# Packed attention and gated feed-forward on one core: a new order of all five queues, and another split of the low-part subtractions between VectorE and GpSimd

## The chip, the cores and the metric

The kernel runs on 1 core of one Trainium2 chip. Its engines are PE (TensorE matmul; PEld is its weight load), DVE (VectorE), ACT (ScalarE), POOL (GpSimd) and SP (SyncE, which issues nearly all DMAs). The metric is the device time of one execution in microseconds (us).

## The reference

Batch 8, 8 heads, 576 rows, head width 64. A pack of 32 queries per head attends to k and v, then every row of q attends to the 32 packed rows; the rows of all heads, 512 wide, go through a feed-forward layer with a gate.

```
p_packed = softmax(p k^T / 8) v          # 32 rows per head
x        = softmax(q p_packed^T / 8) p_packed   # 4608 x 512 over all batches
h        = x @ w_in                      # 512 -> 2048
g        = h * clip(h + 3, 0, 6) / 6
out      = g @ w_out                     # 2048 -> 512
```

The two weights arrive as 64-bit floats, which the kernel reads as pairs of 32-bit words and puts together on the core; q, k, v and p are 32-bit floats.

## The kernel before, in words

**Precision.** A product of two 32-bit matrices is made of three matmuls of rounded parts: high times high, high times low, low times high. So every operand has a high part, which ACT makes by a copy into the rounded type, and a low part, the operand minus its high part, which DVE or POOL makes by a subtraction. `parts_of` (lines 1036 to 1041) issues both, and the table ENGINES names the engine of each subtraction: "D" for DVE, "P" for POOL, and the default of the caller where the table has no entry.

```
def parts_of(hi, lo, x, name, engine="P"):
    nc.scalar.copy(out=hi, in_=x)
    yield
    on(name, engine).tensor_sub(out=lo, in0=x, in1=hi.bitcast(F32))
    yield
```

**Stages.** The start loads k, v, q and p of batch 0 and turns them on PE, makes both attentions of batch 0, and meanwhile reads the weights. Line 404 and line 406 (ACT), line 410 (DVE) and line 414 (POOL) put the two words of a weight block together, 512 columns at a time. The attention comes out as `a_hi` (line 950, ACT) and `a_lo` (line 952, DVE or POOL) for two groups of heads; w_in times the packed rows comes out as `m_hi` and `m_lo` (lines 483 and 485). The first product of the feed-forward layer of batch 0 is line 747: for one block f of 128 hidden units 12 matmuls of 288 columns, six with the parts of group 0 and six with those of group 1, into one pair of PSUM banks (`ps_h`). Only one block has room there at a time: block f+1 starts when the gate of block f has read the banks, by ACT (line 1581, relu of h + 3) and DVE (line 1583, the minimum with 6 times h). The second product is line 997.

Batches 1 to 7 follow. A batch has two halves of 256 or 320 rows. In a half the 16 hidden blocks go in pairs: two first products (line 1019, 6 matmuls each, into one of two PSUM banks in turn), then 7 second products of 3 matmuls each (line 997), which use sums and differences of blocks to save an eighth of the products. Between them stands the gate of each block: line 1030 (ACT) and line 1032 (DVE) read the bank of h and so set it free for the first product after next; then come sums and differences on DVE (lines 1184, 1197, 1203), the high parts on ACT (line 1039) and the low parts on DVE or POOL (line 1041), in the tiles `ge`, `gf`, `ga`. A strip at the edge of a half is kept by POOL (line 1052) and worked off by halves of their own in batches 3 and 7. Beside this the attention of the next batch runs: transposes of q and k on DVE (line 737), scores on PE (line 1347), softmax on ACT and DVE (lines 692 to 714 and 1440), and w_in times the packed rows (line 1449, parts on lines 1455 and 1457). The end of a half combines four accumulators (lines 1233, 1236, 1239, 1246) and stores the rows.

**What sets the order.** Every piece of work is a chain of steps, written as a generator; one step issues one instruction or one group of them. The strings PLAN (batch 0 and the start) and PLANS (batches 1 to 7) name the chain of the next step, word by word: in PLAN `h0` is the first product of block 0, `r0` its gate, `a1` a step of reading w_in for block 1; in PLANS `p14` is a step of pair 4 of the second half, `a14` and `b14` its gates, `z0` a softmax step. Each engine runs its own instructions in the order of that text, so the words also set the order on all five queues. HOMES names the buffer that each tile of four kinds takes.

Of the kernel before, what the change touches and what calls it, by code (L numbers as in the profile page):

```python
# [48 lines left out]
b0 b0 b0 x0 x0 a4 m2 x0 a5 a5 y0 x0 r1 r1 a6 a4 a4 a4 lk0 b6 tk0 li7 m2 m2 m2 r1 r1 a7 a7 a7 h2 h2 a6 a6 y0 x1
a7 x1 r2 r2 x1 lo3 lk1 tk1 h3 h3 b3 a6 r2 r2 tp y2 b5 b5 b5 b5 m4 lk2 y2 x2 b3 b3 b3 r3 x2 tk2 m4 r3 y3 y3 x1  # L50
m4 m4 m4 h4 h4 b5 b5 lo4 b4 li8 r3 r3 b6 b6 b6 li10 x2 b3 b3 r4 r4 a10 x3 x3 x3 a10 a8 lk3 tk3 S b4 b4 x2 x3
a10 S S S S lo8 S h5 h5 b4 below S S b4 b4 r4 li9 r4 y4 y4 y1 y1 x4 x4 lo9 a10 b6 b6 lq0 li11 x4 S S b8 a8 a8
r5 y5 x4 b8 r5 b8 h6 h6 b9 r5 a8 r5 b8 a9 a9 x5 a9 a9 x5 x5 x5 lo7 r6 y6 r6 y6 lq2 h7 h7 a11 a11 a11 b9 y5 tq2
b7 b7 tq0 b7 r6 r6 r7 b8 y7 a11 m8 r7 y7 b8 lo12 b7 m8 m8 m8 b7 S r7 m8 x6 x6 x6 S S S S h8 h8 r8 b9 r7 li13
a13 a13 lq1 tq1 li12 x6 y8 b7 lo10 r8 b9 b9 a13 a13 r8 r8 a12 x7 x7 h9 h9 r9 r9 E E a12 y9 y9 lw0 x7 x7 E a12
b9 b10 b10 y8 E E lq3 li14 a12 tq3 b10 r9 S h10 h10 r10 y10 x8 b10 a14 r10 E E r9 x8 x8 b12 b12 S h11 a14 a14
lv h11 x8 r11 r11 a14 lw1 V r10 x9 b12 b12 b10 y11 V V y11 T T x9 b10 li15 a15 a15 a15 Z Z Z Z Z x9 a15 x9 Z
m12 lo11 b11 b11 b11 r10 x10 b11 m12 m12 m12 y10 m12 lo13 x10 h12 h12 r11 r11 b12 b12 b11 b11 lo14 r12 x10 x10
# [22 lines left out]
-m2 -p12 -b11 -o0 -o0 -p12 -a11 -a11 -p10 -p10 -z0 -b10 -z0 -a12 -a12 -p10 -p10 -p10 -p10 -p10 -p13 -z0 -m2
-a12 -m2 -b12 -z0 -b11 -b11 -b11 -p11 -p11 -m2 -b11 -b11 -b11 -t3 -b11 -z0 -b12 -t1 -a12 -b12 -t3 -t3 -t3 -t3
-t3 -w1 -o0 -p13 -p11 -p11 -p11 -p11 -p11 -a13 -b12 -m2 -z1 -b13 -b12 -b12 -a13 -p12 -b12 -b12 -b12 -s18 -a12
-p12 -b12 -p12 -p12 -a13 -p12 -p12 -p12 -z1 -a13 tk1 -t4 -z1 -g18 -g18 -g18 -a13 -p13 -z1 -b13 -s19 -b13 -m1
-t4 -t4 -g18 -t2 -b13 -b13 -b13 -b13 -b13 -p13 -p13 -z1 -g19 -g19 -m1 -t4 -z1 -b13 -m1 -m1 -b13 -m1 -g19 -s111
-g111 -s110 -t3 -t3 -p13 -g19 -p13 -z1 -p13 -o1 -t4 -t4 -g111 lk0 tk0 -g110 -s18 -g110 -p13 -s113 -w0 -s18 -t5
-t5 -t4 -t4 lq1 -s112 -s19 -s19 -g110 -g110 -o1 -g111 -t5 -t5 -g112 -g112 -t5 -m0 -g112 -s114 -t5 -g111 -z1
-g112 -t5 -s110 -s111 -s110 -m0 -m0 -s111 -t5 -g114 -g114 -z0 -g113 -z0 -o1 -g113 -g113 -s115 -t4 -t4 p05 -t5
-g113 lk2 tk2 -g114 -s112 -s113 -t5 -t5 -t4 a05 -s112 -s113 -t5 -m0 -m0 -g114 -w3 -g115 -g115 -g115 p05 a05
a05 -t5 p04 a05 -o1 -o1 -t5 -t5 -t5 lk3 b05 b05 a05 b05 -s114 -g115 a04 a04 -t5 b05 b05 -s115 a04 -m3 -o1 -t5  # L90
# [1633 lines left out]
```

## Time and profile before

| | |
|---|---|
| Runs | 724.3, 729.7, 723.89 us; median 724.3 |
| Profiled execution | 723.53 us, its span 721.7 us |
| PE busy | 686.5 us, 95% of the span |
| DVE busy | 616.9 us, 85% |
| ACT busy | 433.3 us, 60% |
| POOL busy | 279.7 us, 39% |
| Mean granted clock of PE | 0.986 of full speed |

Busy time is a share of the span; what lies around the span in the profiled execution is 723.53 - 721.7 = 1.8 us. A busy time does not tell whether the work lies on the path that sets the end: that is read from which engine the others wait for in a stretch. The rows are further below.

### The profile page before, as it was taken

The numbers are of one execution on the slowest core, as the hardware profiler recorded it, in microseconds if no ns is written. First come the engines' busy times: TensorE is split into PE (matmuls) and PEld (weight loads), VectorE is DVE, ScalarE is ACT, GpSimd is POOL, SyncE is SP. The second block draws the span as 40 slices with busy tenths as digits, with TensorE's granted clock in tenths as the row PEclk, the third lists the DMA queues.
The fourth block names the chain that finished last, engine by engine and source line by source line (L and its number), as shares of the span: only waits on it lengthen the run. The fifth ranks groups of instructions, "written<-read, shape, count | busy, mean of one in ns | idle before, by whom it ended". The sixth has DMA issues, their size and how long they took to land.

```text
span 721.7 us, 17048 instructions
## 1 busy us (share of the span) xinstructions
PE 686.5 (95%) x6142; PEld 601.1 (83%) x6142; DVE 616.9 (85%) x1495; ACT 433.3 (60%) x1062; POOL 279.7 (39%) x434
## 2 busy tenths in 40 slices
PE   6399999999999999999999999999999999999997
PEld 4277877776878888898998998898989879999996
DVE  2878879699999899979988979997999889788795
ACT  3778966655656556565655656654556655655553
POOL 0345753343322443444323234354322343444332
PEclk9879999999999999999999999999999999999999
DMA  9979942886867459676866875978685845424642
GB/s 224 311 172 238 226 137 74 218 209 203 282 159 190 152 193 298 127 189 189 248 225 178 174 222 173 255 151 213 222 266 122 178 172 193 189 90 151 228 153 82
DMA packets 209156, 138.48 MB, mean 192 GB/s; under 512 B 174256, under 2 KB 186800, under 8 KB 205232
## 3 DMA queue, kind: packets, MB, share of 16 engines
q1 hardware_dynamic: 208800, 137.33, 67.1%
q8 instruction: 48, 0.79, 0.5%
q14 instruction: 36, 0.29, 0.1%
q10 hardware_dynamic: 272, 0.07, 0.0%
HBM read 115.34 MB, written 22.02 MB: 190 GB/s over the span
## 4 chain that ended last, share of the span: by engine, by line
PE 54%; DVE 27%; DMA 6%; ACT 5%; issue 4%; POOL 1%; SPq 1%; DVEq 0%; POOLq 0%; ACTq 0%
PE acc L997 29%; PE h L1019 15%; PE ps_h L747 3%; DVE t L1032 3%; PE at L1449 3%; DVE tr L737 2%; DMA room<-in_q_dram 2%; DVE tb L1032 1%; DVE t L1197 1%; DVE ga L1041 1%; PE at L1347 1%; DVE osb L1239 1%; DVE gf L1041 1%; DVE t L1184 1%; DMA e_again<-e_kept 1%
## 5 line engine op out<-in xcount | busy, mean ns | idle before, releaser
L1019 PE MATMUL h<-a_hi,m_hi 128*128 128x320 f32 (+1 forms) x448 | 138.3, 309 | 6.1 <-DVE t L1032 4.2
L1019 PE MATMUL h<-a_lo,m_hi 128*128 128x320 f32 (+1 forms) x448 | 132.6, 296 | 0.2 <-DVE a_lo L714 0.2
L1019 PE MATMUL h<-a_hi,m_lo 128*128 128x320 f32 (+1 forms) x448 | 132.6, 296 | 0.0
L1019 PEld LDWEIGHTS h<-a_hi,m_hi 128*128 128x128 f32 x448 | 84.8, 189 | 25.9 <-DVE t L1032 10.3
L997 PE MATMUL acc<-wo_hi,ge 128*128 128x256 f32 x456 | 105.8, 283 | 0.1
L997 PE MATMUL acc<-wt,ga 128*128 128x256 f32 x684 | 105.5, 284 | 0.0
L1030 ACT ACTIVATE t<-h,three 128x256 f32<-128x256 f32 (+1 forms) x126 | 63.1, 502 | 56.6 <-PE h L1019 32.5
L997 PEld LDWEIGHTS acc<-wt,ga 128*128 128x128 f32 x684 | 91.9, 191 | 2.8 <-issue 1.7
L1019 PEld LDWEIGHTS h<-a_lo,m_hi 128*128 128x128 f32 x448 | 85.0, 190 | 1.0 <-DVE a_lo L714 0.5
L1019 PEld LDWEIGHTS h<-a_hi,m_lo 128*128 128x128 f32 x448 | 84.7, 189 | 0.3 <-DVE m_lo L1457 0.3
L997 PEld LDWEIGHTS acc<-wo_hi,ge 128*128 128x128 f32 x456 | 80.6, 189 | 5.0 <-issue 2.5
L1039 ACT CAST ga<-t 128x256 fp32r<-128x256 f32 (+1 forms) x114 | 48.1, 422 | 35.4 <-PE acc L997 14.1
L1041 POOL TENSOR_TENSOR ge<-t,ge 128x256 fp32r<-128x256 f32 x57 | 44.9, 788 | 57.1 <-ACT ge L1039 49.8
L1030 ACT ACTIVATE tb<-h,three 128x256 f32<-128x256 f32 (+1 forms) x98 | 49.1, 501 | 29.8 <-PE h L1019 22.7
L1032 DVE SCALAR_TENSOR_TENSOR t<-t,h 128x256 f32<-128x256 f32 (+1 forms) x126 | 55.9, 446 | 12.8 <-ACT t L1030 12.3
L1041 POOL TENSOR_TENSOR ga<-t,ga 128x256 fp32r<-128x256 f32 (+1 forms) x51 | 41.0, 803 | 62.2 <-ACT ga L1039 54.2
L997 PE MATMUL acc<-wo_lo,ge 128*128 128x256 f32 x228 | 63.9, 280 | 0.0
L997 PE MATMUL acc<-wt,gf 128*128 128x256 f32 x342 | 60.3, 285 | 0.2 <-DVE osb L1246 0.2
L997 PE MATMUL acc<-wo_hi,gf 128*128 128x256 f32 x228 | 60.2, 288 | 0.2
L997 PE MATMUL acc<-wo_hi,ga 128*128 128x256 f32 x228 | 59.9, 285 | 0.4 <-DVE ga L1041 0.3
L1039 ACT CAST gf<-tb 128x256 fp32r<-128x256 f32 x98 | 39.7, 405 | 27.0 <-DVE tb L1032 20.3
L1032 DVE SCALAR_TENSOR_TENSOR tb<-tb,h 128x256 f32<-128x256 f32 (+1 forms) x98 | 43.4, 443 | 14.4 <-ACT tb L1030 14.1
(247 smaller groups left out, 1837.0 us busy)
## 6 DMA issues: line engine op xcount, KB each, us to landing
wt<-t_kept SPq DMA_DIRECT2D x41, 768.0 KB, 5.0
w_again<-w_kept SPq DMA_DIRECT2D x24, 1024.0 KB, 5.5
wt<-t_kept SPq DMA_DIRECT2D x39, 256.0 KB, 4.4
nat<-in_k_dram SPq DMA_DIRECT2D x112, 72.0 KB, 4.2
nat<-in_q_dram SPq DMA_DIRECT2D x112, 72.0 KB, 2.9
out_dram<-osb SPq DMA_DIRECT2D x31, 256.0 KB, 2.5
raw_in<-in_moe_w_in_dram SPq DMA_DIRECT2D x10, 512.0 KB, 5.0
raw_out<-in_moe_w_out_dram SPq DMA_DIRECT2D x10, 512.0 KB, 4.9
```

What stands on the lines that cost most here:

```text
L737: nc.vector.transpose(out=t, in_=state.pop(("nat", which, b, a)))
L747: nc.tensor.matmul(h[:, hf, :HS], mm[:, g, fs], aa[:, hf * HS:(hf + 1) * HS], start=(g == 0 and i == 0), stop=(g == NG - 1 and i == 2),)
L997: nc.tensor.matmul(out, lhs[x], rhs[y], start=first and i == 0, stop=last and i == 2, skip_group_check=True)
L1019: nc.tensor.matmul(h, mm[:, g, fs], aa[:, t0:t0 + n], start=(g == 0 and i == 0), stop=(g == NG - 1 and i == 2),)
L1030: nc.scalar.activation(out=t[:, :n], in_=h, func=AF.Relu, bias=three)
L1032: nc.vector.scalar_tensor_tensor(out=t[:, :n], in0=t[:, :n], scalar=6.0, in1=h, op0=ALU.min, op1=ALU.mult)
L1039: nc.scalar.copy(out=hi, in_=x)
L1041: on(name, engine).tensor_sub(out=lo, in0=x, in1=hi.bitcast(F32))
L1184: nc.vector.tensor_sub(out=columns[:, 1, :P], in0=columns[:, 0, P:], in1=columns[:, 0, :P])
L1197: nc.vector.tensor_add(out=columns[:, :, P:], in0=ta[:, off + P:off + P + 2 * (W - P)].rearrange("p (a n) -> p a n", a=2)[:, :, :P], in1=b ...
L1239: nc.vector.scalar_tensor_tensor(out=dst, in0=bank("D")[:, at * H2:at * H2 + H2], scalar=sixth, in1=other, op0=ALU.mult, op1=ALU.add,)
L1449: nc.tensor.matmul(t[x][NPK * a:NPK * a + NPK], pps[b % 2][at, a], w_in_sb[n][at, :, a], start=True, stop=True)
```

## The change

No operation is added and none is removed: PE, ACT and SP keep their instructions, but for one copy more or less between ACT and DVE in the start. What is changed is the four strings of HOMES, the text of PLAN and of all seven PLANS, and the table ENGINES. Two tiles get other names (`at` to `ps_at`, `h` to `ps_h`), which changes nothing that runs. All lines of the program stand 12 lines lower.

On the orders of the two kernels 48 more instructions stand on POOL (439 and 487) and 47 fewer on DVE (1497 and 1450). By the table 149 instructions go from DVE to POOL and 101 from POOL to DVE; net 9 leave DVE in batch 1 and 15 in batch 2. Of those whose number changes, DVE loses net 43 of 256 columns (tiles `ge`, `gf`, `ga`, `g`) and 11 of 128 columns (`ga` from `tb`), and gains 4 of 384 columns; POOL the other way round.

```
 PLAN = """
-in in in in in in in in in li0 p p k2 k0 k2 k0 k1 k3 k3 k1 k5 k5 s0 s0 s0 k4 k4 s1 s1 lo2 s0 e0b s0 s0 e0a q0
+in in in in in in in in in li0 p p k2 k2 k1 k0 k0 k1 s0 s0 s0 k5 k5 k3 k4 s0 e0b e0a k4 k3 s1 e0b e0a v0 s1 s0
...
 PLANS = (
     """
--m2 -m2 -m2 -m2 -m2 s01 lk2 g01 g01 g01 s00 g00 g00 g00 g00 g00 g01 g01 lk1 -m1 kw -m1 -m1 s03 lp s02 tk2 g03
+lk2 lk1 s00 g00 g00 g00 -m1 g00 g00 s01 g01 g01 -m1 kw g01 g01 -m1 -m1 -m1 s02 g01 s00 g02 lp s03 g03 s00 -m2
...
 ENGINES = {
-    "k1": "A", "k3": "D", "p": "A", "er0": "A", "er1": "D", "pp1": "D", "q1": "D", "q3": "A", "k0": "D",
+    "k1": "D", "k3": "D", "p": "A", "er0": "A", "er1": "D", "pp1": "A", "q1": "D", "q3": "A", "k0": "A",
...
-    "P", "s1114": "P", "s1115": "P", "e205": "D", "f205": "D", "g205": "D", "e204": "D", "f204": "D",
+    "P", "s1114": "P", "s1115": "P", "e205": "P", "f205": "D", "g205": "P", "e204": "P", "f204": "P",
...
-        return ps_a.tile([P, 512], F32, name=f"at{x}", tag=f"att{x}")
+        return ps_a.tile([P, 512], F32, name=f"ps_at{x}", tag=f"att{x}")
```

**Place 1: ACT in the start**, from the high part of w_in times the packed rows (`m_hi`) to the first `a_hi`. Before (`raw_in`, `raw_out` and `raw` with a number are weight blocks whose words are put together, `z` is the softmax, `wo_hi` the high part of w_out):

```order
L483 CAST m_hi<-ps_t 128x128
L406 ACTIVATE raw_183<-raw_183 128x512
L938 ACTIVATE z<-z 128x576
L424 CAST wo_hi<-x_out 128x512
L404 ACTIVATE raw_in<-raw_in 128x512
L406 ACTIVATE raw_in<-raw_in 128x512
L938 ACTIVATE z<-z 128x288
L404 ACTIVATE raw_out<-raw_out 128x512
L406 ACTIVATE raw_out<-raw_out 128x512
L404 ACTIVATE raw_out<-raw_out 128x512
L406 ACTIVATE raw_out<-raw_out 128x512
L950 CAST a_hi<-room 128x576
```

Now, with lines 416, 418, 950, 962 and 495 for 404, 406, 938, 950 and 483:

```order
L495 CAST m_hi<-ps_t 128x128
L416 ACTIVATE raw_out<-raw_out 128x512
L950 ACTIVATE z<-z 128x288
L418 ACTIVATE raw_375<-raw_375 128x512
L416 ACTIVATE raw_out<-raw_out 128x512
L418 ACTIVATE raw_out<-raw_out 128x512
L962 CAST a_hi<-room 128x576
L962 CAST a_hi<-room 128x288
```

The exponential of 576 columns of group 0 has moved out of this piece, to in front of the first weight block; from the start of the kernel to the first `a_hi` 12 conversions of lines 404 and 406 and one `wo_hi` stood on ACT, now 11 and none. The two groups' `a_hi` follow each other.

**Place 2: PE at the first product of batch 0**, with the engines that an instruction waits for. Before:

```order
L747 MATMUL ps_h_428<-a_hi,m_hi 128x288 [waits PE_49,Activation_49]
L747 MATMUL ps_h_428<-a_lo,m_hi 128x288 [waits DVE_49]
L747 MATMUL ps_h_428<-a_hi,m_lo 128x288 [waits DVE_49]
L747 MATMUL ps_h_428<-a_hi,m_hi 128x288
L747 MATMUL ps_h_428<-a_lo,m_hi 128x288
L747 MATMUL ps_h_428<-a_hi,m_lo 128x288
L472 MATMUL ps_t<-w_in_sb_331,pp_212 32x128 [waits Pool_49]
L472 MATMUL ps_t<-w_in_sb_331,pp_212 32x128 x7
L747 MATMUL ps_h_428<-a_hi,m_hi 128x288 [waits Activation_49]
```

Now:

```order
L759 MATMUL ps_h_413<-a_hi,m_hi 128x288 [waits DVE_49,PE_49,Activation_49]
L759 MATMUL ps_h_413<-a_lo,m_hi 128x288 [waits Pool_49]
L759 MATMUL ps_h_413<-a_hi,m_lo 128x288 [waits DVE_49]
L759 MATMUL ps_h_413<-a_hi,m_hi 128x288
L759 MATMUL ps_h_413<-a_lo,m_hi 128x288
L759 MATMUL ps_h_413<-a_hi,m_lo 128x288
L759 MATMUL ps_h_413<-a_hi,m_hi 128x288 [waits Activation_49]
L759 MATMUL ps_h_413<-a_lo,m_hi 128x288 [waits DVE_49]
L759 MATMUL ps_h_413<-a_hi,m_lo 128x288 [waits DVE_49]
```

The product of w_in with the packed rows for block 1 (line 472, 16 small matmuls) stood between the two halves of the first product, and now stands behind it; the wait for `a_lo` of group 0 has gone from DVE to POOL.

**Place 3: DVE at the change of halves in batch 6**, before (`osb` is an evicted output, `t` and `tb` on lines 1032 and 1044 the gates that free a bank of `h`):

```order
L1032 SCALAR_TENSOR_TENSOR tb<-tb,h_1537 128x320
L1197 TENSOR_TENSOR t<-t,tb 128x2x128
L1203 TENSOR_TENSOR tb<-tb,t 128x128
L1041 TENSOR_TENSOR gf<-tb,gf 128x256
L1239 SCALAR_TENSOR_TENSOR osb<-acc,osb 128x256
L1032 SCALAR_TENSOR_TENSOR t<-t,h_1536 128x320
L1184 TENSOR_TENSOR t<-t 128x128
```

Now:

```order
L1209 TENSOR_TENSOR t<-t,tb 128x2x128
L1215 TENSOR_TENSOR tb<-tb,t 128x128
L1053 TENSOR_TENSOR gf<-tb,gf 128x256
L1452 STREAM_TRANSPOSE z<-ps_at_8549 128x512
L1452 STREAM_TRANSPOSE z<-ps_at_8550 128x512
L1044 SCALAR_TENSOR_TENSOR tb<-tb,ps_h_1537 128x320
L704 TENSOR_REDUCE mx_8608<-z 128x18
L706 TENSOR_TENSOR z<-z,mx_8608 128x576
L1196 TENSOR_TENSOR t<-t 128x128
L1251 SCALAR_TENSOR_TENSOR osb<-acc,osb 128x256 x3
```

Before, one eviction (line 1239) stood between the sums of a pair and the next gate; now two transposes of the softmax (line 1452, before 1440) stand there, and the evictions come after that gate.

## Rows read from the trace of the kernel before

**Rows 1.** The page: busy time by engine, and PE's granted clock in 40 slices.

```profile
PE 686.5 (95%) x6142; PEld 601.1 (83%) x6142; DVE 616.9 (85%) x1495; ACT 433.3 (60%) x1062; POOL 279.7 (39%) x434
...
PEclk9879999999999999999999999999999999999999
```

**Rows 2.** Windows of 20 us: stretch, length, busy us and instructions by engine, clock, DMA.

```profile
0.00:20.00 20.00, 13.35 (x154) 9.28 (x155) 5.43 (x16) 6.53 (x14) 0.96 (x7) 1.00 0.98 240
20.00:40.00 20.00, 8.73 (x123) 5.63 (x121) 16.94 (x40) 14.80 (x29) 8.93 (x8) 0.73 0.92 276
40.00:60.00 20.00, 18.71 (x114) 14.55 (x113) 16.20 (x31) 16.02 (x30) 8.85 (x7) 0.84 0.75 185
...
180.00:200.00 20.00, 18.74 (x153) 16.87 (x153) 19.90 (x49) 13.72 (x35) 8.17 (x12) 1.00 0.89 274
700.00:720.00 20.00, 16.50 (x138) 16.29 (x137) 12.55 (x29) 8.12 (x22) 5.87 (x9) 0.97 0.34 115
```

**Rows 3.** Waits of PE: waiter, releaser, us in total, times, longest.

```profile
PE ps_h L747 <- ACT a_hi L950: 8.4, 1, 8.4
PE h L1019 <- DVE t L1032: 4.2, 7, 1.0
PE h L1019 <- DVE tb L1032: 1.5, 2, 1.1
```

**Rows 4.** Timeline of the start: start us, duration us, engine, line, operation, wait before it.

```profile
21.50 0.76 DVE L936 TENSOR_TENSOR z<-z,mx 128x576 f32<-128x576 f32 x1
...
27.51 0.68 ACT L938 ACTIVATE z<-z 128x576 f32<-128x576 f32 x1
...
33.26 0.67 ACT L950 CAST a_hi<-room 128x576 fp32r<-128x576 f32 x1 [0.18 <-DVE room L948]
...
33.96 1.58 DVE L952 TENSOR_TENSOR a_lo<-room,a_hi 128x576 fp32r<-128x576 f32 x1
...
33.98 0.61 PE L747 MATMUL ps_h<-a_hi,m_hi 128*128 128x288 f32 x1 [8.38 <-ACT a_hi L950]
...
35.60 0.61 PE L747 MATMUL ps_h<-a_lo,m_hi 128*128 128x288 f32 x1 [1.01 <-DVE a_lo L952]
...
36.66 0.61 PE L747 MATMUL ps_h<-a_hi,m_lo 128*128 128x288 f32 x1 [0.45 <-DVE m_lo L485]
...
38.52 0.61 PE L747 MATMUL ps_h<-a_hi,m_hi 128*128 128x288 f32 x1
...
40.37 0.74 ACT L1581 ACTIVATE t<-ps_h,three 128x576 f32<-128x576 f32 x1 [1.81 <-PE ps_h L747]
```

**Rows 5.** Groups by form: line, engine, operation, count, busy us, mean ns, idle before.

```profile
L404 ACT ACTIVATE raw_in<-raw_in 128x512 f32<-128x512 f32 x10 | 6.8, 678 | 1.9 <-DMA raw_in<-in_moe_w_in_dram 1.9
```

**Rows 6.** Groups by form: the subtractions on either engine, a sum, a transpose.

```profile
L1197 DVE TENSOR_TENSOR t<-t,tb 128x256 f32<-128x256 f32 x98 | 45.7, 466 | 2.1
...
L1041 POOL TENSOR_TENSOR ga<-t,ga 128x256 fp32r<-128x256 f32 x45 | 34.9, 774 | 55.4 <-ACT ga L1039 47.3 <-DVE den L703 2.9 <-DVE m_lo L1457 2.8
...
L1041 DVE TENSOR_TENSOR ga<-t,ga 128x256 fp32r<-128x256 f32 x53 | 24.8, 470 | 2.1 <-ACT ga L1039 2.0
...
L1041 POOL TENSOR_TENSOR ga<-tb,ga 128x128 fp32r<-128x128 f32 x51 | 26.3, 515 | 39.8 <-ACT ga L1039 28.2 <-PE h L1019 3.2 <-PE at L1449 2.6
...
L1041 DVE TENSOR_TENSOR ga<-tb,ga 128x128 fp32r<-128x128 f32 x47 | 17.3, 369 | 0.7 <-ACT ga L1039 0.5
...
L1440 DVE STREAM_TRANSPOSE z<-at 128x512 f32<-128x512 f32 x12 | 8.0, 696 | 0.8 <-PE at L1347 0.5
```

**Rows 7.** Timeline: line 1197 alone, then beside a GpSimd instruction.

```profile
186.67 0.42 DVE L1197 TENSOR_TENSOR t<-t,tb 128x256 f32<-128x256 f32 x1
...
590.35 0.74 POOL L1236 TENSOR_TENSOR osb<-osb 128x256 f32<-128x256 f32 x1 [0.93 <-ACT osb L1233]
...
590.38 0.99 DVE L1197 TENSOR_TENSOR t<-t,tb 128x256 f32<-128x256 f32 x1
...
593.36 0.41 PE L1019 MATMUL h<-a_hi,m_hi 128*128 128x320 f32 x1 [1.05 <-DVE t L1032]
```

More of the change, by code (lines that the diff above doesn't have):

```diff
@@ L49 @@
[L49 to L58, printed above, removed]
@@ new lines @@
+x2 b3 y3 h4 h4 b5 b5 lo4 b4 li8 r3 r3 b6 b6 b6 li10 x2 b3 b3 r4 r4 a10 lk3 y4 y4 a8 y1 x2 a8 y1 tk3 a8 x3 x3
+a10 b4 a8 li9 b4 b4 S lo8 lq1 S S S r4 S S S x3 x3 S b4 r4 h5 a9 h5 b4 x4 a10 S S r5 a10 li11 x4 r5 b8 x4 S b8
+below b8 h6 lo7 b8 S S r5 a9 a9 h6 x4 a11 r6 tq1 a9 r5 x5 a11 r6 lo9 b6 y5 y5 b8 r6 a11 x5 S x5 b6 b7 S b7 lq2
+tq2 b7 h7 h7 r7 a11 r7 x5 m8 m8 m8 m8 m8 lo10 r6 r7 b7 y6 y6 b7 b9 r7 x6 b7 b9 b9 x6 h8 h8 r8 y7 y7 y8 li13
+a13 x6 x6 b9 a13 r8 x7 b8 b10 lq3 tq3 a13 E r8 r8 E y8 a13 li12 h9 h9 E E E E x8 r9 r9 lo12 b9 lq0 tq0 b9 a12
@@ L63 @@
+r15 r14 Z Z x13 x13 b15 b15 x14 Z x14 r15 r15 r15 x14 x15 Z Z Z Z Z x15 x15 o0 o0 M o2 o2 x14 x15 Z Z y15
+stage M M M o1 o1 o3 o3 M y15
 """
@@ L81 @@
[L81 to L90, printed above, removed]
@@ new lines @@
+lw0 V V p10 S V V V g013 f00 g013 p00 p00 p00 p00 p00 t6 a10 t6 t6 p00 Z g013 g013 a10 Z Z Z Z z0 -o1 s012 t7
+t7 o0 o0 t7 s015 p00 s012 g015 g015 g015 s013 s013 -ek a10 t7 t7 t7 z1 g015 z0 p10 a10 t7 t7 a10 a10 t6 o0 o0
+p11 w2 t7 t6 t6
+    """,
+    """
+lk3 -t7 -z1 -b10 -b10 -m2 -b10 lk0 -o0 -z0 -s014 -s014 -w1 -s015 -s015 -b10 -a11 -a11 -t6 -t6 -t6 -t6 -a11 -o0
+-a11 -b10 -b10 -b10 -b10 -b10 -p11 -b11 -b10 -o0 -b11 -o0 -b10 -p10 -b11 -z0 -p16 -z1 -m2 -o0 -p10 -p10 -a11
+-a11 -a16 -a16 -p16 -m2 -p10 -p10 -p10 -p10 -b16 -b16 -f12 -a16 -a16 -p17 -z1 -b11 -b16 -b11 -z0 -z0 -z1 -m2
@@ new lines @@
+b15 a14 a14 a14 a14 z0 p14 b14 b14
+    """,
+    """
+lk0 tk0 -p05 -a15 -a15 -o0 -m0 -p05 -m0 -m0 -m0 -o0 -b15 -o0 -o0 -o0 -w3 -b15 -p05 -p05 -o0 -o0 -a14 -p05 -o0
+-b15 -b15 -b15 -a14 -p13 -b14 -p13 -a13 -a13 -p15 -p15 -p15 -a13 -p15 -b14 -b14 -b14 -b14 -p15 -b13 -p15 -b14
+-p15 -z1 -p14 -p14 -p14 -a13 -m0 -b13 -p12 -z0 -p12 -z0 -b14 -a13 -a13 -b14 -b14 -p14 -p14 -p14 -m3 -p14 lp
+-b13 -z0 -z0 -a12 -b13 -z0 -b13 -b13 -b13 -b13 -b13 -b13 -b13 lk3 -z1 -o0 -a12 -a12 -f17 -b12 -b12 tp -w1 -m3
+-a12 -b12 -p13 -p13 -b12 -b12 -b12 -b12 -p17 -m3 -p13 -a17 -p17 -m3 -p13 -m3 -a12 -p12 -a12 -p13 -p13 -p12
@@ new lines @@
+b05 b05 b05 b05 p04 p04 a15 p15 p04 p04 a05 a05 p05 b05 b05 b15 b15 a15 b15 b15 b15 z0 z0 b15 b15 b15 a15 p14
+a14 p05 o0 o0 z0
+    """,
+    """
+lk0 -m0 tk0 -p14 -b14 lk2 -p05 -p05 -p05 -p05 -a14 -p05 -w3 -o0 -o0 -b14 -p13 -p13 -a15 -o0 -m0 -o0 -p15 -p15
+-a14 -a13 -a13 -p15 -b15 -b15 -p15 -o0 -o0 -p15 -p15 -p15 -a14 lk1 -z0 -f17 -b14 -b14 -b14 -b14 -b14 -b14 -b14
+-m0 -p12 -m0 -m0 -a14 -b13 -b14 -b13 -a13 -b13 -b13 -b13 -b13 -b13 -b13 -b13 tk2 -b13 -p14 -p14 -p14 -p14 -p14
+-p14 -f16 -a12 -a12 -p12 -m3 -a12 -b12 -b12 -p14 -z1 -a13 -b12 -b12 -b12 -a12 -a12 -a13 -p13 -w1 -m3 -p13 -p13
@@ L232 @@
+a14 b14 b14 p13 b14 b14 b14 b14 b14 b14 b13 b13 p13 p13 p13 p13 p13 a15 a15 f15 a14 a14 b15 b15 a15 b15 b15
+b15 b15 p14 p14 p14 f14 p14 p14 p14 p14 b15 b15 a15 a15 p15 p15 p15 p15 p15 b15 b15 p15 p15 o1 o1 o1 o1 o1 o1
+o1 o1 o1
     """,
@@ L1679, in packed_attention_moe @@
         ps_h = ctx.enter_context(tc.tile_pool(name="ps_h", bufs=1, space=bass.MemoryType.PSUM))
-        hh = [ps_h.tile([P, 512], F32, name=f"h{x}") for x in range(2)]
+        hh = [ps_h.tile([P, 512], F32, name=f"ps_h{x}") for x in range(2)]
         ps_a = ctx.enter_context(tc.tile_pool(name="ps_a", bufs=1, space=bass.MemoryType.PSUM))
```

307 lines of the change are left out of this document (150 added, 157 removed), and 103 rows, old and new, of the table ENGINES.

## The prediction

> **What bounds the kernel now.** I read the page first, then stretches of 20 us, then the waits of PE, then the timeline where they lie. The page [rows 1] says PE: busy 686.5 of 721.7 us, so that 35.2 us of the span are all that an order can win from PE's idle time. The stretches [rows 2] say where these lie. The first three leave PE idle for 6.65, 11.27 and 1.29 us, together 19.2. The last one leaves 3.50, and 1.7 us of span lie behind it; that is the last accumulators being evicted and stored, which this change leaves as it is. The rest, 35.2 - 19.2 - 3.5 - 1.7 = 10.8 us, is spread over the 640 us between. Of the waits by name [rows 3], one in the start takes 8.4 us: the first matmul of line 747 waits for `a_hi`. Nine later ones, 4.2 us in seven and 1.5 us in two, wait for line 1032, the gate on VectorE that frees a bank of h. VectorE is the second engine: 616.9 us by the page, and 19.90 of 20 us in the worst stretch [rows 2]. GpSimd has 279.7 us. So there are two things to win: an earlier first product, and fewer gates that come late because VectorE is behind.
>
> After that idle time PE ran for a while at the lower of its two levels, 1.2 GHz: the granted clock is 0.73 and 0.84 in the second and third stretch, and 1.00 in the one before [rows 2]. That time follows the idle time, so I count no gain of its own for it.
>
> **The change, part 1: the start.** In the trace [rows 4] group 0's differences are ready at 21.50 + 0.76 = 22.26 us, but ACT takes their exponential only at 27.51, behind conversions of weights. `a_hi` starts at 33.26 and `a_lo` ends on VectorE at 33.96 + 1.58 = 35.54. PE has its first matmul at 33.98, the second at 35.60, the third, which needs `m_lo`, at 36.66, and the second group's six matmuls from 38.52 on; the gate starts at 40.37. In the new order the exponential stands in front of all conversions, and ahead of `a_hi` stand 11 conversions and no `wo_hi`, where there were 12 and one. By their duration of 678 ns [rows 5] these two are at most 1.36 us; consecutive ones overlap a little, so I take 1.2: `a_hi` starts at 32.1 and ends at 32.8. `a_lo` of this group is moved to GpSimd. The trace shows no such instruction of 576 columns there; one of 256 takes 774 ns [rows 6], so 576/256 of that, 1.74 us, is my price from above, and the 1.58 us that VectorE took [rows 4] the one from below. So `a_lo` ends at about 34.5, 1.0 us earlier. `m_lo` now stands on VectorE ahead of the second group's softmax, so the wait before 36.66 goes. Each group's six matmuls take 40.37 - 38.52 = 1.85 us at that clock. Without block 1's small matmuls between the groups, the gate can start at 34.5 + 2 x 1.85 = 38.2, which is 2.2 us earlier than 40.37.
>
> What then comes late is ACT and VectorE: the conversion and the cast that were left behind must be made before the next blocks. So the gain is 0 if these are paid in the stretch of 40 to 60 us, where ACT and VectorE are busy for about 16 of 20 us each [rows 2] and have room, and 3 us if the second group is no later than the first. I take 2.
>
> **Part 2: the subtractions.** Net, VectorE gives up 43 of 256 columns at 470 ns and 11 of 128 at 369 ns [rows 6], 20.2 + 4.1 us; the few of other sizes take back some 2 us. VectorE so loses 22 us. GpSimd takes 43 x 0.774 + 11 x 0.515 = 38.9 us, less about 4 for the long ones, 35 in all, and is busy for 315 us, 13% more. None of this is on PE's path by itself: on the order, between a first product and the products that use its low parts there lies other PE work in both kernels. The cover is this distance; where it is gone, a low part on GpSimd comes 0.774 - 0.470 = 0.3 us later [rows 6].
>
> There is a price. Line 1197 takes 0.42 us alone, and 0.99 us when a GpSimd instruction of 0.74 us has started just before it [rows 7]. Its mean is 466 ns [rows 6], so it pays 46 ns on average. If every one of VectorE's some 1,495 instructions paid that, it would be 69 us, and 13% more of GpSimd would add 9; if only the 98 of line 1197 did, 0.6. Most of VectorE's work here are sums of two SBUF tiles like line 1197, the others not; I take 4. That leaves VectorE 18 us lighter (13 to 21), which is 2.7% of its span.
>
> What that buys PE is bounded by the nine waits for gates, 5.7 us [rows 3], from above. A mean load does not end them: they come from local pile-ups, such as a lock, an eviction and the next gate in a row. The third place of the order shows one such pile-up exchanged for another: before, one eviction in front of the gate; now two transposes of 696 ns [rows 6]. From below I allow a loss of the same size, 6 us. I take a gain of 2, a third of what there is, since VectorE gets less to do everywhere.
>
> **The sum.** 723.5 (the profiled execution) - 2 - 2 = 719.5 us. The median of the runs shown is 724.3, 0.8 above the profiled execution; that is less than the runs differ by, so the forecast for the median stays at 719.5 to 720.3, and I write **720**. A measurement of this kernel can tell about 1% from no change, which is 717.1 and 731.5.
>
> **The rivals.** (B) *The lock in front of the gates.* The worst late gate of the trace is of this kind: line 1197 is held by GpSimd until 591.37, the gate behind it comes late, and PE waits 1.05 us at 593.36 [rows 7]. With GpSimd busier by 13%, and with new pile-ups at new places, more gates are hit. Each costs PE up to 1.05 us. From four on, the gain of both parts is gone; with nine more, twice as many as now, the time is 720 + 9.5 = 729.5. For it: locked instructions are easy to find in the trace. Against it: VectorE is 18 us lighter, and PE's waits are few today although such locks are many.
>
> The Trainium skill, page "SBUF — State Buffer", section "Who interferes with whom", has a rule that speaks against this change: a VectorE instruction with two SBUF inputs contends with a GpSimd instruction that reads SBUF, and the one that comes later is blocked for the other's whole instruction. The row of 0.99 us agrees with that. By the rule taken literally a VectorE instruction would wait, on average, GpSimd's share times half an instruction of 774 ns, that is 0.39 x 0.39 = 0.15 us, three times the 46 ns of the mean; five points more of GpSimd would then add 0.02 us to each of VectorE's instructions, at most 29 us, more than the 22 us that are taken off it. That is rival B with VectorE as the bound, at the 729.5 us worked out above.
>
> (C) *The start gives its gain back.* The gate of block 0 comes 2 us earlier, but block 1 waits for conversions that were left behind, and by 60 us PE is where it was; the later waits stay. Then the time is 723.5 to 724. For it: ACT and VectorE were the chain through this stretch too. Against it: both have 4 us of room there [rows 2].
>
> (D) *Both go as far as they can.* 3 us in the start, and all nine gate waits with their share of the smaller ones, 6 to 7 us: 723.5 - 9.5 = 714. For it: by the table net 9 and 15 instructions leave VectorE in batches 1 and 2, and the stretch of 180 to 200 us [rows 2] lies there. Against it: the pile-up at the third place.
>
> **How the numbers follow.** The forecast, 720 with its own range of 717 to 723, has 0.45; C has 0.17; D 0.18; B 0.20. D is under 717.1 with nearly all it has, and the lower end of the forecast adds 0.05 to that: faster by over 1%, 0.23. B is over 731.5 with half or a little more: slower by over 1%, 0.12. The rest, 0.65, is within 1%. The range runs from 714, which leaves out half of D, to 729, which leaves out half of B: together 0.19 left out.
>
> **What would show it.** Right: the first matmul of line 759 (747 before) at about 33 us and the gate of block 0 at about 38; PE idle in the first three stretches down from 19.2 to 17; VectorE at about 599 us and GpSimd at 315; the waits for the gates (line 1044) at 3 to 4 us. Wrong in part 1: the second block of line 759 starts as late as before, with waits for ACT. Wrong in part 2: line 1209 (1197 before) with a mean well above 470 ns, and more than nine waits for gates. Wrong altogether: new waits of PE for `ge`, `gf` or `ga` from GpSimd, which hardly exist today, or a PE that is busy for other than 686 us.

## The result, and the profile after

The new kernel takes 700.2 us (median, 698.96 to 701.07). The kernel before took 727.0 us beside it (723.89 to 729.91). The ratio is 0.963, 95% interval 0.958 to 0.969. In the profiled executions the span falls from 721.7 to 699.4 us, by 22.3; the rest of the difference of the medians is that the kernel before spreads over 6 us and was profiled at its low end, and the new one at its high end (701.07). The forecast was 720 us, with 714 as the lower end.

The page of the kernel after, the lines that answer to [rows 1], and the chain of work that ended last, by engine:

```profile
span 699.4 us, 17112 instructions
PE 672.9 (96%) x6142; PEld 598.9 (86%) x6142; DVE 591.7 (85%) x1448; ACT 429.0 (61%) x1061; POOL 312.3 (45%) x482
...
PEclk9779999999999999999999999999999999999999
...
PE 81%; DMA 8%; DVE 5%; ACT 2%; issue 2%; SPq 1%; POOL 0%; DVEq 0%; POOLq 0%; ACTq 0%
```

The same chain before, in which VectorE has 27% where it has 5% now:

```profile
PE 54%; DVE 27%; DMA 6%; ACT 5%; issue 4%; POOL 1%; SPq 1%; DVEq 0%; POOLq 0%; ACTq 0%
```

PE runs the same 6,142 matmuls and is "busy" for 13.6 us less. Its idle time falls by only 8.7 us, from 35.2 to 26.5. So most of the gain lies where the page showed work. VectorE is at 591.7 us (forecast 599) and GpSimd at 312.3 (forecast 315).

The stretches of 20 us after, columns as in [rows 2]:

```profile
0.00:20.00 20.00, 13.27 (x156) 9.06 (x157) 6.10 (x17) 6.36 (x13) 0.96 (x7) 1.00 0.99 248
20.00:40.00 20.00, 9.17 (x137) 6.07 (x134) 18.41 (x40) 14.53 (x30) 9.72 (x7) 0.64 0.90 265
40.00:60.00 20.00, 18.99 (x122) 15.32 (x122) 17.80 (x34) 18.25 (x35) 13.88 (x14) 0.94 0.94 226
...
180.00:200.00 20.00, 19.43 (x147) 16.16 (x146) 19.04 (x42) 12.76 (x31) 10.90 (x15) 1.00 0.84 210
```

The first three leave PE idle for 6.73 + 10.83 + 1.01 = 18.6 us; it was 19.2, and I had said 17. The timeline of the start after, against [rows 4]:

```profile
32.86 0.61 PE L759 MATMUL ps_h<-a_hi,m_hi 128*128 128x288 f32 x1 [5.95 <-ACT a_hi L962]
...
32.88 1.42 POOL L964 TENSOR_TENSOR a_lo<-room,a_hi 128x576 fp32r<-128x576 f32 x1
...
34.35 0.61 PE L759 MATMUL ps_h<-a_lo,m_hi 128*128 128x288 f32 x1 [0.89 <-POOL a_lo L964]
...
36.91 0.61 PE L759 MATMUL ps_h<-a_hi,m_hi 128*128 128x288 f32 x1 [0.99 <-ACT m_hi L495]
...
38.76 0.74 ACT L1593 ACTIVATE t<-ps_h,three 128x576 f32<-128x576 f32 x1 [0.80 <-PE ps_h L759]
```

The gate of block 0 starts at 38.76 us, 1.6 earlier than the 40.37 before; I had worked out 38.2. How much of this is the new order, other traces tell further below. `a_lo` on GpSimd took 1.42 us, less than my lower bound of 1.58, but the second group waited for an `m_hi`.

**Where the time was hidden.** The timeline of PE before, at the place where `tb` frees a bank (start, duration, and in brackets the idle time before):

```profile
185.04 0.28 PE L997 MATMUL acc<-wo_hi,ge 128*128 128x256 f32 x1
185.16 0.28 PE L997 MATMUL acc<-wo_lo,ge 128*128 128x256 f32 x1
185.28 0.29 PE L997 MATMUL acc<-wo_hi,ge 128*128 128x256 f32 x1
186.69 0.38 PE L1019 MATMUL h<-a_hi,m_hi 128*128 128x256 f32 x1 [1.12 <-DVE tb L1032]
186.91 0.28 PE L1019 MATMUL h<-a_lo,m_hi 128*128 128x256 f32 x1
187.03 0.28 PE L1019 MATMUL h<-a_hi,m_lo 128*128 128x256 f32 x1
```

Matmuls of 256 columns start every 0.12 us, but each record lasts 0.28: it goes on 0.16 us past the start of the next. So behind such a matmul a wait of up to 0.16 us leaves PE "busy", and a longer one shows 0.16 too little. On top, the matmul behind the late one starts 0.22 us after it, not 0.12. Without a wait the late one would have started at 185.28 + 0.12 = 185.40, so the wait of 1.12 us in the brackets cost 186.69 - 185.40 + 0.10 = 1.39 us.

Lost time can be counted without the ends of records. I take the time from each matmul's start to the next one's, and for each line and shape the lower quartile of these as its pace. The paces add up to 591.5 us before and 592.2 after; what intervals have above them is lost: 119.0 us before, 95.8 after, a difference of 23.2. The difference is what counts: some 25 us of either sum stand behind the small matmuls of line 1449, which start eight at a time within 0.05 us, with 0.4 to 0.5 us to whatever follows, and are the same in both kernels. Of the 23.2, 2.6 us lie in the first 60 us. After 60 us the first products (line 1019, where they follow another first or second product) go from 15.9 to 4.3, second products behind second products from 13.0 to 10.3, and the rest gives 6. Of the 20.6 us after 60 us, 8.1 were visible as idle PE (16.0 before, 7.9 after) and 12.5 were not.

The waits of the weight loads (PEld) show the same, and were there to be read. Before, over the whole span (waiter, releaser, us in total, times, longest):

```profile
PEld h L1019 <- DVE t L1032: 10.3, 17, 1.3
...
PEld h L1019 <- DVE tb L1032: 5.4, 11, 1.3
```

and after:

```profile
PEld ps_h L1031 <- DVE tb L1044: 2.2, 3, 0.8
PEld ps_h L1031 <- DVE t L1044: 2.1, 3, 0.8
```

28 gates and 15.7 us, where PE's own waits [rows 3] had nine and 5.7. After there are six and 4.3. PE's own waits for the gates, of the kernel after:

```profile
PE ps_h L1031 <- DVE tb L1044: 0.3, 1, 0.3
PE ps_h L1031 <- DVE t L1044: 0.2, 1, 0.2
```

I call a gate late if it ends less than 0.15 us before the first matmul that needs its bank. By starts and ends in the traces 31 of 222 were late before, and 3 are after.

### The profile page after: what moved, and what is told of

It reads as the page before. It is cut to its first block, busy times and chain, and to the rows that moved or that the text cites. A ratio compares the mean times of both kernels' runs of the same rounds, so it can differ in the third digit from the quotient of the medians.

```text
span 699.4 us, 17112 instructions
## 1 busy us (share of the span) xinstructions
PE 672.9 (96%) x6142; PEld 598.9 (86%) x6142; DVE 591.7 (85%) x1448; ACT 429.0 (61%) x1061; POOL 312.3 (45%) x482
## 4 chain that ended last, share of the span: by engine, by line
PE 81%; DMA 8%; DVE 5%; ACT 2%; issue 2%; SPq 1%; POOL 0%; DVEq 0%; POOLq 0%; ACTq 0%
PE acc L1009 45%; PE ps_h L1031 24%; PE ps_at L1461 4%; PE ps_h L759 3%; DMA wt<-t_kept 2%; DMA nat<-in_q_dram 2%; PE ps_at L1359 1%; DMA raw<-in_moe_w_out_dram 1%; DMA w_again<-w_kept 1%; PE ps_at L1433 1%; DMA e_again<-e_kept 1%; DMA p_nat<-in_p_dram 1%; PE ps_w L848 1%; SPq L505 1%; PE ps_t L820 1%
## 5 line engine op out<-in xcount | busy, mean ns | idle before, releaser
L1031 PE MATMUL ps_h<-a_hi,m_hi 128*128 128x320 f32 (+1 forms) x448 | 135.5, 303 | 0.5 <-DVE tb L1044 0.3
L1031 PE MATMUL ps_h<-a_hi,m_lo 128*128 128x320 f32 (+1 forms) x448 | 132.8, 296 | 0.1
L1031 PE MATMUL ps_h<-a_lo,m_hi 128*128 128x320 f32 (+1 forms) x448 | 132.5, 296 | 0.0
L1042 ACT ACTIVATE t<-ps_h,three 128x256 f32<-128x256 f32 (+1 forms) x126 | 63.1, 502 | 66.3 <-PE ps_h L1031 44.4
L1031 PEld LDWEIGHTS ps_h<-a_hi,m_hi 128*128 128x128 f32 x448 | 85.0, 190 | 17.4 <-DVE tb L1044 2.2
L1031 PEld LDWEIGHTS ps_h<-a_lo,m_hi 128*128 128x128 f32 x448 | 84.9, 190 | 1.0
L1031 PEld LDWEIGHTS ps_h<-a_hi,m_lo 128*128 128x128 f32 x448 | 84.8, 189 | 0.5 <-DVE m_lo L741 0.5
L1053 POOL TENSOR_TENSOR ga<-t,ga 128x256 fp32r<-128x256 f32 (+1 forms) x66 | 52.1, 789 | 49.1 <-ACT ga L1051 30.4
L1042 ACT ACTIVATE tb<-ps_h,three 128x256 f32<-128x256 f32 (+1 forms) x98 | 49.1, 501 | 37.7 <-PE ps_h L1031 30.0
L1044 DVE SCALAR_TENSOR_TENSOR t<-t,ps_h 128x256 f32<-128x256 f32 (+1 forms) x126 | 56.1, 446 | 17.8 <-ACT t L1042 16.1
L1051 ACT CAST ga<-t 128x256 fp32r<-128x256 f32 (+1 forms) x114 | 47.8, 420 | 22.3 <-PE acc L1009 9.7
L1044 DVE SCALAR_TENSOR_TENSOR tb<-tb,ps_h 128x256 f32<-128x256 f32 (+1 forms) x98 | 43.6, 445 | 11.9 <-ACT tb L1042 11.4
```

Source lines behind the costliest of these rows:

```text
L1031: nc.tensor.matmul(h, mm[:, g, fs], aa[:, t0:t0 + n], start=(g == 0 and i == 0), stop=(g == NG - 1 and i == 2),)
L1042: nc.scalar.activation(out=t[:, :n], in_=h, func=AF.Relu, bias=three)
L1044: nc.vector.scalar_tensor_tensor(out=t[:, :n], in0=t[:, :n], scalar=6.0, in1=h, op0=ALU.min, op1=ALU.mult)
```

## The experiments

VectorE and GpSimd are busy us of the profiled execution. Each ratio is to the kernel before as measured beside that run, which took 727.0 to 728.8 us. "Blocked" is what VectorE's instructions after 60 us last beyond the lower quartile of their shape, counting those with over 0.1 us.

| run | order | split | us | ratio to before, 95% interval | VectorE | GpSimd | blocked | late gates |
|---|---|---|---|---|---|---|---|---|
| before | old | old | 727.0 | | 616.9 | 279.7 | 50 | 31 |
| after | new | new | 700.2 | 0.963 (0.958 to 0.969) | 591.7 | 312.3 | 37 | 3 |
| e1_order | new | old | 734.6 | 1.010 (1.006 to 1.013) | 613.7 | 280.1 | 48 | 15 |
| e2_split | old | new | 751.0 | 1.032 (1.029 to 1.035) | 607.9 | 315.4 | 55 | 29 |
| e3_start | new start, old rest | same | 725.3 | 0.998 (0.996 to 1.001) | 617.2 | 283.9 | 49 | 30 |
| e4_rest | old start, new rest | same | 705.2 | 0.970 (0.966 to 0.974) | 590.5 | 307.1 | 37 | 2 |
| e5_backD | new | new, 140 back on VectorE | 721.9 | 0.990 (0.985 to 0.995) | 621.0 | 216.6 | 29 | 14 |
| e6_backP | new | new, 93 back on GpSimd | 709.5 | 0.973 (0.969 to 0.978) | 581.7 | 378.5 | 56 | 5 |
| e7_toP | old | old, 140 to GpSimd | 734.7 | 1.008 (1.005 to 1.011) | 585.1 | 373.2 | 58 | 26 |
| e8_toD | old | old, 93 to VectorE | 740.2 | 1.015 (1.009 to 1.020) | 628.1 | 215.5 | 33 | 32 |
| noP_before | old | no low parts on GpSimd | 716.8 | 0.986 (0.982 to 0.990) | 580.2 | 114.6 | 10 | 19 |
| noD_before | old | no low parts on VectorE | 717.6 | 0.986 (0.982 to 0.991) | 527.7 | 272.4 | 31 | 19 |
| noP_after | new | no low parts on GpSimd | 699.8 | 0.962 (0.957 to 0.966) | 563.3 | 117.9 | 9 | 2 |
| noD_after | new | no low parts on VectorE | 700.3 | 0.963 (0.959 to 0.967) | 529.9 | 307.9 | 34 | 0 |
| e13_hoist | old, 21 gates ahead | old | 727.0 | 1.000 (0.997 to 1.003) | 614.6 | 278.3 | 48 | 19 |
| e14_hoist_noD | same | no low parts on VectorE | 716.9 | 0.986 (0.982 to 0.990) | 527.1 | 272.0 | 31 | 13 |
| e15_noLow_before | old | no low parts | 713.5 | 0.980 (0.977 to 0.984) | 505.3 | 114.3 | 8 | 12 |
| e16_noLow_after | new | no low parts | 701.2 | 0.964 (0.961 to 0.967) | 504.5 | 117.5 | 9 | 1 |

### Order alone, split alone

e1_order is the new kernel with the old table, e2_split the old kernel with the new one:

```
 ENGINES = {                                   # e1_order; e2_split the other way round
-    "e205": "P", "f205": "D", "g205": "P", "e204": "P", "f204": "P",
+    "e205": "D", "f205": "D", "g205": "D", "e204": "D", "f204": "D",
...
```

> The new order of all queues with the old split of the low parts (the old table ENGINES). Between the two traces the idle time of the weight loads behind VectorE fell from 36.8 to 20.7 us, and 31 gates before and 3 after ended less than 0.15 us ahead of the first product that needed their bank. Theory T, the places of the gates in VectorE's order did it: this kernel takes 701 to 706 us, VectorE is back at about 615 us busy, and at most 8 gates end that late. Rival R1, the 25 us taken off VectorE did it: 716 to 722 us, with 20 or more such gates. Rival R2, order and split work only as a pair: 722 us or more.

> The old order with the new split (the new table ENGINES). Theory T: 720 to 727 us, VectorE at about 593 us busy and still 20 or more gates that end less than 0.15 us ahead of the first product that needs their bank. Rival R1: 704 to 712 us. Rival R2: 724 us or more, since the low parts that go to GpSimd come later than the old order allows for.

My theory fell: 734.6 and 751.0 us. Either half alone is slower than the kernel before, by 1% and 3%, and the pair is 3.7% faster. Load alone (R1) fell with it. R2 was right for both. Where e1_order loses is in PE's waits (its line numbers are two less than before):

```profile
PE ps_h L1017 <- DVE t L1030: 4.5, 8, 1.3
PE acc L995 <- DVE ge L1039: 4.2, 4, 1.8
...
PE acc L995 <- DVE ga L1039: 2.2, 3, 1.3
```

The second products (`acc`) wait for low parts that the new order expects from GpSimd and that now stand in VectorE's queue. By the starts of matmuls 31.2 us are lost between second products, against 10.3 in the new kernel. e2_split waits for gates (line 1039 there) and for low parts:

```profile
PE h L1026 <- DVE t L1039: 8.1, 11, 1.7
...
PE acc L1004 <- DVE gl L1597: 3.6, 1, 3.6
PE h L1026 <- DVE tb L1039: 2.5, 5, 1.2
...
PE acc L1004 <- POOL ge L1048: 1.3, 4, 0.6
```

By the starts, its first products lose 21.4 us (15.9 in the kernel before) and its second products behind second products 28.5 (13.0 before), so more of its loss lies between second products than at the gates. On its page VectorE's busy time, the same instructions as in the new kernel, is 16 us longer than there:

```profile
PE 692.0 (92%) x6142; PEld 602.0 (80%) x6142; DVE 607.9 (81%) x1448; ACT 430.7 (57%) x1061; POOL 315.4 (42%) x482
```

### Start alone, rest alone

The text PLAN and the entries of the start from the one kernel, PLANS and the other entries from the other; HOMES follows the text.

```
 # e3_start: the old kernel with
+PLAN = <new>;  HOMES["t"][:16], HOMES["g"][:32] = <new>
 # e4_rest: the new kernel with
+PLAN = <old>;  HOMES["t"][:16], HOMES["g"][:32] = <old>
```

> The new order and split up to the end of batch 0 (PLAN), the old ones for batches 1 to 7 (PLANS). At the same amount of PE's work the new kernel was ahead of the old one by 1.9 us at 50 us, 3.7 us at 105 us and 10.7 us at 180 us. If the parts simply add: 719 to 721 us against some 724 for the kernel before. Rival, the start's gain is given back in batches 1 and 2, because the same late gates wait there for something else than the start: 723 to 725 us.

> The old order and split up to the end of batch 0, the new ones for batches 1 to 7. If the parts add: 703 to 706 us. Rival, the gain in batch 1 (7 us between 105 and 180 us of the old kernel's time) rests on what the new start leaves behind: 710 to 713 us.

e4_rest is 705.2 us, as the sum of parts says: the rest gives 22 us and the start some 5 more, though the intervals of the two ratios overlap. e3_start is 725.3: its gain cannot be told from none. By its trace it was 3.5 us ahead of the old kernel at 120 us and 2.3 at 200, and lost this again, 1.6 us of it at one wait for a transfer that landed only 0.6 us earlier than in the old kernel:

```profile
PE acc L982 <- DMA wt<-t_kept: 1.5, 1, 1.5
```

So with the old rest my rival C fits, although a gain of 3 us is not excluded there; that the new rest keeps more of the start's gain is likely and not shown.

### The moves by direction

```
 # e5_backD: new ENGINES, the 140 D->P entries set to "D"   e6_backP: the 93 P->D entries set to "P"
 # e7_toP:   old ENGINES, the 140 set to "P"                e8_toD:   the 93 set to "D"
```

> The new kernel with the 140 subtractions of batches 1 to 7 that went to GpSimd back on VectorE; the 93 that came the other way stay there too. VectorE then carries about 140 x 0.44 = 62 us more than in the new kernel, some 653 us. Theory L, what counts is VectorE's load (the lighter it is, the fewer late gates): slower than the new order with the old split, 740 us or more, with more than 15 late gates. Theory M, each low part must be on the engine whose queue has room at its place in that text: 718 to 735 us, about as far from the new kernel as the 140 are a share of all 233 moves, and second products that wait for `ge`, `gf` and `ga` from VectorE.

> The new kernel with the 93 subtractions that came to VectorE back on GpSimd; the 140 stay there too. VectorE has about 41 us less than in the new kernel, some 550 us, GpSimd some 65 us more, 380 us. Theory L: 694 to 702 us, no slower than the new kernel. Theory M: 710 to 725 us, with second products that wait for low parts from GpSimd although VectorE has never had so little to do.

> The old kernel with only the 140 moved from VectorE to GpSimd. VectorE some 555 us, GpSimd some 385 us. Theory L: 700 to 712 us, the late gates down from 31 to under 10. Theory M: 740 us or more, because the old text puts the second products too close behind these low parts; late gates then go down but waits for low parts from GpSimd come up.

> The old kernel with only the 93 moved from GpSimd to VectorE. VectorE some 658 us. Theory L: 745 us or more, with more late gates than the 31. Theory M: 735 to 750 us, by gates and by low parts from VectorE that come late.

Theory M holds in direction in all four; e6_backP is half a us under its range and e7_toP 5 us. In these two VectorE is busy for 10 and 32 us less than in the kernel that they start from, and both are slower than that kernel, by 9 us (7 by the ratios) and 6 us. Against L that decides. In e5_backD the waits of PE are for low parts on VectorE first, then for gates:

```profile
PE acc L1005 <- DVE ge L1049: 4.1, 3, 2.0
PE acc L1005 <- DVE gf L1049: 2.6, 6, 0.7
PE ps_h L1027 <- DVE t L1040: 2.4, 5, 1.3
```

These four also show how little of a move comes back as free time of VectorE. Its busy time changed by 29.3 us for 140 instructions (e5_backD), 10.0 for 93 (e6_backP), 31.8 for 140 (e7_toP) and 11.2 for 93 (e8_toD): 0.11 to 0.23 us each, where an instruction lasts 0.37 to 0.47 [rows 6]. The traces give two reasons. Neighbouring records on VectorE overlap: before, 1,081 instructions start some 0.08 us ahead of the end of the one in front, 86.0 us in all, and busy time counts such a moment once. And there is the company of GpSimd. In e7_toP the moved records were 62.5 us; 15.1 us of overlap went with them, and VectorE's other records became 15.5 us longer. In the four runs the other records changed against the move by 11.3, 19.7, 15.5 and 12.7 us, where the moved ones were 55.4, 37.4, 62.5 and 30.4: a fifth to a half. The sum of two tiles shows it: its mean [rows 6] is 429 ns with GpSimd at 215 us and 497 ns with GpSimd at 373 us. These two rows are from e8_toD and from e7_toP:

```profile
L1203 DVE TENSOR_TENSOR t<-t,tb 128x256 f32<-128x256 f32 x98 | 42.0, 429 | 2.0
```

```profile
L1195 DVE TENSOR_TENSOR t<-t,tb 128x256 f32<-128x256 f32 x98 | 48.7, 497 | 2.2
```

No gate shows a block. Line 1032 before (min, median, max ns) has nothing above 490, and of 256 columns, `tb` included, nothing above 423:

```profile
L1032 DVE SCALAR_TENSOR_TENSOR t<-t,h x126: 360/446/490, 128.8 to 711.0; 128x320 f32<-128x320 f32 x64, 128x256 f32<-128x256 f32 x62
```

A gate reads one operand from PSUM. The Trainium skill, page "SBUF — State Buffer", section "Who interferes with whom", says that a VectorE instruction with at most one SBUF input, outside VectorE's two-port modes, does not contend with GpSimd; the row agrees. In the new pair GpSimd's instructions overlap 175 us of such VectorE work after 60 us (133 before) and 108 us of sums and subtractions of two SBUF tiles (124 before), by starts and ends of the records. That fits with 37 us blocked and not 50, with a busier GpSimd; no run changes this overlap alone, so it is not shown to be the cause.

### Low parts left out

```
+    def low_of(hi, lo, name, engine="P"):
+        return hi if on(name, engine) is nc.gpsimd else lo     # noD: nc.vector
...
-        on(name, engine).tensor_sub(out=lo, in0=x, in1=hi.bitcast(F32))
+        if low_of(hi, lo, name, engine) is lo:
+            on(name, engine).tensor_sub(out=lo, in0=x, in1=hi.bitcast(F32))
...
-            lhs[part] = hi[:, k], lo[:, k]
+            lhs[part] = hi[:, k], low_of(hi, lo, name)[:, k]
```

> The old kernel without the 237 low parts of batches 1 to 7 that GpSimd makes (169 us of GpSimd): the second products take the high part in their place, so PE does the same matmuls. VectorE keeps every instruction; only what GpSimd did to it is gone. In the old kernel VectorE's instructions that last over 0.1 us longer than usual for their shape add up to 50 us after 60 us; I expect some 15 here and VectorE at 580 us. Theory K, blocked VectorE instructions are a main part of why gates come late: 706 to 714 us, under 15 late gates instead of 31. Rival, the old order itself puts the gates too late, blocked or not: 718 to 725 us, 22 or more late gates.

> The old kernel without the 242 low parts of batches 1 to 7 that VectorE makes (118 us of VectorE); GpSimd keeps its own. If VectorE's lateness is all that separates old from new after the start: 702 to 707 us, under 8 late gates. If the old text costs PE something that VectorE has no part in: 710 us or more with VectorE at 500 us.

> The new kernel without the 284 low parts that GpSimd makes there (202 us). Blocked time of VectorE from 37 to some 12 us. By theory K the new text has few late gates left to win: 695 to 700 us. Rival, the new kernel still loses to blocked instructions what its traces hide: 690 us or less.

> The new kernel without the 195 low parts that VectorE makes there (84 us). 694 to 699 us: 3 late gates are all that VectorE still costs. Rival as above: 690 us or less.

The old order gains 10 to 11 us from either, and keeps 19 late gates: noP_before lies between theory K and its rival, noD_before with those who gave the old text a loss of its own. The new order gains nothing (noD_after is just above its range), although VectorE is busy for 62 us less in noD_after:

```profile
PE 670.9 (96%) x6142; PEld 598.2 (86%) x6142; DVE 529.9 (76%) x1248; ACT 428.3 (61%) x1061; POOL 307.9 (44%) x482
```

So the low parts of either engine cost the old kernel 10 to 11 us, and the new one nothing that can be told.

### Gates put ahead, and no low parts at all

```
 # e13_hoist: PLANS of the old kernel, 21 places like this one
-... -m1 -m1 s03 lp s02 tk2 g03 g03 g02 ...
+... -m1 -m1 s03 g03 g03 lp s02 tk2 g02 ...
 # e14_hoist_noD: the same, and low_of as above for VectorE; e15, e16: low_of returns hi always
```

> The old kernel, old split, with 21 of its 31 late gates moved ahead by up to two VectorE instructions (14 of them with the ACT step of the gate ahead by up to two ACT instructions); nothing else is touched. PE loses 7.6 us at these 21 places by the trace, and some 0.1 us more at the next matmul each. Theory Q, these gates are late because of what stands ahead of them on VectorE and ACT, and what was ahead can wait: 715 to 720 us, some 12 late gates instead of 31. Rival S, there is no slack to give: what is passed (high parts, low parts, evictions) is then late for the second products or the next gates: 722 to 730 us, with new waits of second products.

> The same 21 gates moved, and the 242 low parts that VectorE makes left out (the high part takes their place in the products). Without the moves that kernel takes 717.6 us. If the places of the gates and VectorE's load are two separate losses: 708 to 712 us. If the late gates were VectorE's load only: 716 to 719 us.

> The old kernel without any low part of batches 1 to 7, on either engine. If load and blocking add up: 705 to 710 us. If the old text keeps a loss that neither engine's low parts cause: 712 to 717 us.

> The new kernel without any low part of batches 1 to 7: 697 to 700 us, as with either engine's low parts gone; under 695 us would say that the two together still cost something.

e13_hoist answers for rival S: the late gates go from 31 to 19 and 4.3 of the 15.9 us at first products are won, but 2.5 us come up between second products and some 1 in attention, and the time stays at 727.0. One of the new waits:

```profile
PE acc L997 <- DVE gf L1041: 1.0, 1, 1.0
```

Without VectorE's low parts the moves give nothing either (716.9 against 717.6), though the late gates go from 19 to 13. The number of late gates alone does not set the time. With no low part at all the old order stays at 713.5 and the new one at 701.2, a little over what I expected of it. 12 us therefore separate the two orders with neither these subtractions nor a difference in blocking (8 and 9 us). By the starts of matmuls some 6 us of them lie within attention (lines 1347 and 1421 in the old numbering), 1.6 in the start, and 1 at first products; the rest I did not trace to a place. Between the two full kernels these lines of attention differ by only some 1 us, so the 12 us are no fixed share of the 22 that the pair gives.

## Why the prediction was wrong

**The step that failed** is the bound of part 2: "What that buys PE is bounded by the nine waits for gates, 5.7 us, from above", and ahead of it "35.2 us of the span are all that an order can win from PE's idle time". Both take PE's busy record for work. After 60 us the order won 20.6 us where the page showed 16.0 us of idle PE in all. The first products that wait for gates alone gave some 12 us, and 12.5 us in all came out of time that the page called busy. The sign "a PE that is busy for other than 686 us" was the one that fired, with 672.9. The Trainium skill, page "Perfetto Trace Analysis", section "Identifying Performance Opportunities", says that matmul busy time is not a good measure of how close PE is to its limit, and to use instead the share of its peak rate that is reached and the busy share of weight loads. The trace agrees: weight loads were busy for 83% in the line of [rows 1], 120.6 us idle, and 86% after, 100.5 us idle. These 20.1 us are nearly the whole gain. The reason that the section gives, that pipelined instructions look smaller in the trace, does not hold here: a record of 0.28 us stands for 0.12 us of pace.

**Part 1, the start:** right in direction, and smaller than forecast as far as the traces tell. The gate came 1.6 us earlier (2.2 forecast), but the trace of the kernel before is the latest of its kind: in nine traces with the old start (before, e4_rest, e7_toP, e8_toD, noP_before, noD_before, e13 to e15) it starts at 38.94 to 40.37 us, median 39.77, and in seven with the new one at 38.41 to 39.26, median 38.76. That is 1.0 us. PE was 1.9 us ahead of the trace before at 50 us, but so are the other traces with the old start, by 1.2 to 2.1; at 60 us those are 1.2 to 1.7 us ahead, and the ones with the new start 2.3 to 3.4. In the new order the new start is worth some 5 us (700.2 against 705.2 in e4_rest, with intervals that overlap), where I allowed 3 at most; in the old order nothing that can be told (e3_start).

**Part 2, VectorE's relief:** VectorE fell by 25 us where I had 18, and GpSimd rose by 33 where I had 35, but the argument behind was wrong. The 22 us are lengths of records, of which a part overlaps with the neighbours: with the old order (e2_split) VectorE is busy for only 9 us less, the overlap having shrunk by 7.7. My price of blocking, 4 us, was about right there (the blocked time goes from 50 to 55); in the new order there was none to pay (37). And "VectorE gets less to do everywhere" is not what helps: less on VectorE made both orders slower (e6_backP, e7_toP).

The 18 us are also not 2.7% of the span but 2.5% (2.9% of VectorE's busy time), and the late gate that I called the worst, with 1.05 us, is second to the one of 1.12 us shown above; nothing hangs on either. The sum of [rows 6], of the kernel after, by form:

```profile
L1209 DVE TENSOR_TENSOR t<-t,tb 128x256 f32<-128x256 f32 x98 | 46.3, 472 | 2.3
```

Its mean is 472 ns against 466: the sign that I had named for rival B's lock, "well above 470 ns", did not come.

**The third place of the order** and the "pile-ups" were judged by what stands ahead of a gate. e13_hoist shows that this can't be read one gate at a time: what is passed is late next.

**What I conclude:** the gain belongs to order and split as a pair. That is shown, by both being slower alone; "order" here takes in the buffers of HOMES, which no run changes by themselves. Where PE's time was lost and is not lost now is shown by the starts of its matmuls. That the pair wins because gates end in time, low parts are ready, and GpSimd works beside VectorE's PSUM reads fits the counts, but no run holds one of these alone, and fewer late gates by themselves gained nothing (e13_hoist). Which of the many moved steps carry the gain, and the 12 us that separate the orders without low parts, stays open.

## What to carry to other kernels

Bound what an order can win by the idle time of the weight loads, or by the starts of matmuls against their pace, not by PE's idle time: at 95% busy there were still 22 us in it. These bounds are loose: the new kernel still has 100.5 us of the one and 95.8 of the other. Compare such a number only with the spread of several traces of the same code: the start of one kernel differed by over 1 us between executions. An assignment of work to two engines and the order of their queues are one decision; test a new split only with the order made for it. Here a subtraction moved to GpSimd freed a quarter to a half of its own length on VectorE; gates, which read PSUM, were not slowed by GpSimd, and sums of SBUF tiles were.

## What the runs showed of the hardware

- A late matmul makes the next one late too, by some 0.10 us: 56 times before and 29 times after at the second matmul of a first product, and each time that the first one came over 0.05 us late.
- Neighbouring instructions of VectorE overlap by some 0.08 us in the records, 1,081 times before: 702.9 us of records make 616.9 us of busy time.
- After the small matmuls of line 1449 (64 rows by 32 columns) the next matmul of full size starts 0.52 us after the last of them, 27 times in either kernel. The next eight of the same line start 0.41 us after it, 26 times. The Trainium skill, page "TensorEngine Tiling (Array Packing)", says that a change of tiling mode drains TensorE; of the 27 intervals before, of 0.519 to 0.536 us, at most the 0.11 us above 0.41 can be put down to that, no more than a late matmul costs anyway, so no run here shows the drain by itself.
- Taking 62 us of busy time off VectorE, or 194 off GpSimd, left the new kernel where it was (noD_after, noP_after): what two engines at 85% and 45% spent on these subtractions cost PE nothing that can be told.
